# Low words of the first weight's float64 numbers: the shift moved from VectorE to ScalarE

## Chip, core and metric

The kernel runs on one core of a Trainium2 chip. Its engines are TensorE (PE, with PEld for its weight loads), VectorE (DVE), ScalarE (ACT), GpSimd (POOL) and SyncE (SP, which here only issues DMAs). The metric is the device time of one execution in microseconds (us), as the median of several runs; smaller is better.

## What is computed

Causal attention with a bias from a running sum, then two dense two-layer blocks, each 512 to 2048 to 512 wide, over 2304 tokens:

```python
x = attention(q, k, v, s)                 # 4 batches, 8 heads, 576 tokens, head size 64
x = x.transpose(0, 2, 1, 3).reshape(2304, 512)
h = x @ moe_w_in;   x = (h * tanh(log1p(exp(h)))) @ moe_w_out
h = x @ moe2_w_in;  return (h * sigmoid(1.702 * h)) @ moe2_w_out
```

The four weight matrices are handed over as float64. Chip engines work in float32 here, so every weight has to be converted on the core from its two 32-bit words.

## The kernel before

**Stages.** The attention is cut into steps, each for some heads of one tile of 128 queries. `tick()` writes one step: scores on TensorE (L328, L333), their minimum with the bias on VectorE (`do_max`, L346), the exponential on ScalarE (`do_exp`, L358, shown as L112 because the helper `lut` records it), a high and a low half (`do_hilo`, L372 on ScalarE, L373 on VectorE), a transposing DMA (L377), and four steps later the product with v on TensorE (L397, L401). While the attention goes on, the matmuls of the first layer (L581 to L583, `first_layer`) are mixed in for each 256 tokens that are ready. They need the first weight, `moe_w_in`. After the attention come the second layer, then the second block's two layers.

**Loading a weight.** `load_w` is called 16 times for each of the four matrices, once for each 128 columns (or rows). One call issues one DMA of 512 KB into a raw tile `wst` (L543 for an "in" weight). The raw tile is seen as pairs of 32-bit words: `zi` is the low word of each float64, `yi` the high word, `y` the high word read as float32; each is 128 x 512 with a stride of two. For the first weight (`sided` is true) the steps are:

- L562, ScalarE (shown as L112 with the tile wst): the high word is scaled by 2^-112, with a Prelu whose slope for negative numbers sets the sign apart.
- L565, VectorE: the low word is shifted right by 29 bits, so that three bits are left.
- L566, VectorE: the high word is shifted left by three and joined with these three bits.
- L576, ScalarE: the high half of the weight, `th`. L577, GpSimd: the low half, `tl_`, by a subtraction.

The three other weights are not `sided`; they take a Copy (L564) in the place of the Prelu and one more VectorE step (L570). 

**Order.** All engines take their instructions in order. The order on each engine and the buffers are drawn up by a planner when the program is built, and it works from its own model of what each instruction costs (`schedule_with_timeline_sim=True`). The first weight's DMAs are kept behind the transposing DMA written just ahead of them (L547, L548). The 16 loads of the first weight are started by `bg_a`, from `tick` loops and from `first_layer`. Raw tiles of this stage come from the same five buffers (`mo_a`, tag `hs`) that hold the first layer's output on its way to memory.

Of the kernel before, what the change touches and what calls it, by code (L numbers as in the profile page):

```python
# [13 lines left out]
AF = mybir.ActivationFunctionType  # L14
ALU = mybir.AluOpType
# [36 lines left out]
def attention_moe_moe_kernel(  # L52
# [12 lines left out]
    nc = tc.nc  # L65
# [9 lines left out]
    scale = 1.0 / math.sqrt(D)  # L75
# [35 lines left out]
    def lut(out, in_, func, **kw):  # L111
        i = nc.scalar.activation(out=out, in_=in_, func=func, **kw)  # L112
        if gate_ins[0] is not None:
            tc.add_manual_dep(i.ins, gate_ins[0].name, order, reason="table set")
        since.append(i.ins)
        return i
# [11 lines left out]
    def tmp_pair(dt, nm):  # L128
        tmp_n[0] += 1
        p = mo_a if mo_b[0] is None or tmp_n[0] % (MA + MBB) < MA else mo_b[0]  # L130
        return p.tile([128, 1024], dt, tag="hs", name=nm)
# [396 lines left out]
    def load_w(pool, stage, lay, m, kind):  # L528
        t = pool.tile([128, 2, DM], F32R, tag="w", name="w")
        if stage:  # L530
            rt = stage.tile([128, 1024], F32, tag="wst", name="wst", bufs=NRAW)
        else:
            rt = tmp_pair(F32, "wst")
        if wide:
            rv = rt.bitcast(I32)
            r = rv.rearrange("p (f two) -> p f two", two=2)
            src = (w1_in, w2_in, w1_out, w2_out)[lay + 2 * (kind == "out")].bitcast(I32)
        else:
            rv = r = rt[:, 0:DM]
            src = (w1_in, w2_in, w1_out, w2_out)[lay + 2 * (kind == "out")]  # L540
        if kind == "in":
            n = src.shape[1] // NF
            ld = nc.sync.dma_start(  # L543
                out=rv.rearrange("p (c f) -> p c f", c=KC),
                in_=src[:, m * n:(m + 1) * n].rearrange("(c p) f -> p c f", p=128),
            )
            if lay == 0 and last_pt[0] is not None:  # L547
                tc.add_manual_dep(ld.ins, last_pt[0].ins.name, order, reason="weights behind transposes")  # L548
            win_t[lay, m] = t
        else:  # L550
            nc.sync.dma_start(out=rv, in_=src[m * 128:(m + 1) * 128, :])
            wout_t[lay, m] = t
        th, tl_ = t[:, 0, :], t[:, 1, :]
        if not wide:
            nc.scalar.activation(out=th, in_=r, func=AF.Copy)
            nc.vector.tensor_tensor(out=tl_, in0=r, in1=th, op=ALU.subtract)
            return
        zi, yi = r[:, :, 0], r[:, :, 1]
        y = yi.bitcast(F32)
        sided = lay == 0 and kind == "in"  # L560
        if sided:
            lut(y, y, AF.Prelu, scale=2.0 ** -112, alpha=-(2.0 ** 32))  # L562
        else:
            nc.scalar.activation(out=y, in_=y, func=AF.Copy, scale=2.0 ** -112)  # L564
        nc.vector.tensor_scalar(out=zi, in0=zi, scalar1=29, scalar2=None, op0=ALU.logical_shift_right)  # L565
        nc.vector.scalar_tensor_tensor(  # L566
            out=yi if sided else zi, in0=yi, scalar=3, in1=zi, op0=ALU.logical_shift_left, op1=ALU.bitwise_or
        )
        if not sided:
            nc.vector.scalar_tensor_tensor(  # L570
                out=yi, in0=yi, scalar=-(2 ** 31), in1=zi, op0=ALU.bitwise_and, op1=ALU.bitwise_or
            )
        if lay == 0 and kind == "out":
            nc.gpsimd.tensor_scalar(out=th, in0=y, scalar1=1.0, scalar2=0.0, op0=ALU.mult, op1=ALU.add)  # L574
        else:
            nc.scalar.activation(out=th, in_=y, func=AF.Copy)  # L576
        nc.gpsimd.tensor_tensor(out=tl_, in0=y, in1=th, op=ALU.subtract)  # L577
# [7 lines left out]
    def l1_mm(ps, lay, m, xr, first):  # L585
# [15 lines left out]
        out=maskb, in_=maskb, pattern=[[-1, 128]], compare_op=ALU.is_ge, fill=BIG, base=0, channel_multiplier=1  # L601
    )
    nc.gpsimd.memset(maskp, 0.0)
    for a in range(2):
        nc.gpsimd.affine_select(
            out=maskp[64 * a:64 * a + 64], in_=maskp[64 * a:64 * a + 64], pattern=[[-1, 64]],
# [16 lines left out]
    def bg_a():  # L623
        if wq:
            load_w(wa_p, None, 0, wq.pop(0), "in")
# [41 lines left out]
    def bg_w(pool, stage, lay, m, kd):  # L667
        return lambda: load_w(pool, stage, lay, m, kd)
# [76 lines left out]
    for m in range(NF):  # L745
# [7 lines left out]
        if m % 2:  # L753
            nc.sync.dma_start(
                out=h_d[:, m - 1:m + 1, (NU - UE) * U:NT], in_=t.rearrange("p (m t) -> p m t", m=2)
# [11 lines left out]
    for i, (u, t0, W, m0, n) in enumerate(groups1):  # L767
# [20 lines left out]
        if m0 + n == NF:  # L788
            k_ = 512 // W
            for e in range(KC * W // 512):  # L790
# [4 lines left out]
                for p in range(2):  # L795
                    nc.sync.dma_start(
                        out=x2_d[:, p, cs, t0:t0 + W],
                        in_=x2[:, p].bitcast(F32).rearrange("p (c t) -> p c t", c=k_),
# [105 lines left out]
```

## Time and profile before

| | |
|---|---|
| Median of 3 runs | 1065.03 us |
| Lowest, highest run | 1063.39 us, 1070.41 us |
| Profiled execution, its own time | 1066.92 us |
| Its span, first to last instruction | 1065.1 us |
| Granted TensorE clock, mean over the span | 0.962 |
| Busy: PE, DVE, ACT, POOL | 999.0, 557.4, 484.5, 273.3 us |

The profile is of one execution. Its time is 1.82 us more than its span. Times in the trace are counted from the start of the span. Busy time of an engine is the time in which it ran at least one instruction; the granted clock is a share of full speed, so 0.50 is the lower of TensorE's two levels, 1.2 GHz, and 1.00 is 2.4 GHz.

### The profile page before, as it was taken

Reading aid. Unit: us, or ns where it says so; the run is one execution under the profiler, and the core shown is the slowest. Engines: PE = TensorE matmul, PEld = TensorE weight load, DVE = VectorE, ACT = ScalarE, POOL = GpSimd, SP = SyncE. Lnnn points to the kernel's source line nnn. Section 1 sums busy time; section 2 is a strip of 40 time slices with the busy share of each in tenths; the row PEclk is TensorE's granted clock in tenths of the full one; section 3 lists DMA queues with packets and bytes.
Section 4 is the critical chain, followed back from the end, with each engine's and each line's share of the span. In section 5 each row is a group of like instructions: output and inputs, shape, how many; then the busy total and the mean of one; then the engine's idle time right before and its main releaser. Section 6 shows DMA issues by size and latency. Waiting matters only on the chain.

```text
span 1065.1 us, 16948 instructions
## 1 busy us (share of the span) xinstructions
PE 999.0 (94%) x6396; PEld 865.6 (81%) x6396; DVE 557.4 (52%) x1074; ACT 484.5 (45%) x1010; POOL 273.3 (26%) x307
## 2 busy tenths in 40 slices
PE   3688899989999999999999979899999999999998
PEld 3577798888989889987888869688888888888897
DVE  5798786674557863576534575662222222222231
ACT  4778777584658862463212343442222222222121
POOL 3445532341124112655232254220000100100000
PEclk7679899989999999999999989899999999999999
DMA  9899987996699796797533656520300300210010
GB/s 231 161 251 277 258 208 172 231 188 161 139 222 219 146 196 198 251 382 276 178 119 119 194 166 195 158 80 6 114 1 0 99 20 1 60 40 1 20 40 20
DMA packets 192562, 154.35 MB, mean 145 GB/s; under 512 B 117921, under 2 KB 161953, under 8 KB 192481
## 3 DMA queue, kind: packets, MB, share of 16 engines
q1 hardware_dynamic: 182240, 131.25, 46.6%
q0 software_dynamic: 10240, 22.03, 8.1%
q8 instruction: 50, 0.82, 0.3%
q14 instruction: 32, 0.25, 0.1%
HBM read 93.92 MB, written 33.10 MB: 119 GB/s over the span
## 4 chain that ended last, share of the span: by engine, by line
PE 55%; DMA 10%; DVE 5%; POOL 3%; issue 2%; ACT 2%; SPq 0%; ACTq 0%; POOLq 0%; DVEq 0%
PE acc L844 18%; PE h L581 9%; PE h L582 9%; PE h L583 9%; DMA wst<-in_moe_w_out_dram 3%; DMA wst<-in_moe_w_in_dram 2%; POOL w L577 2%; PE s L328 2%; DVE wst L570 2%; PE acc L583 2%; PE acc L582 2%; PE acc L581 2%; DMA hg<-h_d 2%; DVE wst L566 1%; PE o L397 1%
## 5 line engine op out<-in xcount | busy, mean ns | idle before, releaser
L581 PE MATMUL h<-xh,w 128*128 128x256 f32 (+1 forms) x768 | 252.5, 331 | 8.5 <-DVE z L831 5.1
L582 PE MATMUL h<-xh,w 128*128 128x256 f32 (+1 forms) x768 | 248.4, 324 | 0.0
L583 PE MATMUL h<-xh,w 128*128 128x256 f32 (+1 forms) x768 | 246.9, 322 | 0.0
L844 PE MATMUL acc<-w,gh 128*128 128x512 f32 x576 | 177.8, 390 | 0.0
L581 PEld LDWEIGHTS h<-xh,w 128*128 128x128 f32 x768 | 147.6, 193 | 21.3 <-DVE z L831 5.5
L582 PEld LDWEIGHTS h<-xh,w 128*128 128x128 f32 x768 | 148.1, 193 | 10.8
L583 PEld LDWEIGHTS h<-xh,w 128*128 128x128 f32 x768 | 147.5, 192 | 10.5 <-POOL w L577 0.2
L831 DVE TENSOR_TENSOR z<-h,sg 128x512 f32<-128x512 f32 x72 | 49.7, 690 | 193.1 <-ACT sg L112 192.7
L112 ACT ACTIVATE sg<-h 128x512 f32<-128x512 f32 x72 | 42.9, 596 | 204.2 <-PE h L583 204.2
L844 PEld LDWEIGHTS acc<-w,gh 128*128 128x128 f32 x576 | 107.6, 188 | 21.7
L582 PE MATMUL acc<-gl,w 128*128 128x512 f32 (+1 forms) x320 | 120.1, 375 | 4.0 <-DVE gl L717 4.0
L581 PE MATMUL acc<-gh,w 128*128 128x512 f32 (+1 forms) x320 | 119.7, 374 | 3.1 <-POOL w L574 1.7
L577 POOL TENSOR_TENSOR w<-wst,w 128x512 fp32r<-128x512 f32 x64 | 90.6, 1418 | 116.7 <-ACT w L576 115.6
L583 PE MATMUL acc<-gh,w 128*128 128x512 f32 (+1 forms) x320 | 117.6, 374 | 0.7 <-POOL w L577 0.7
L844 PE MATMUL acc<-w,gl 128*128 128x512 f32 x288 | 112.2, 389 | 0.0
L112 ACT ACTIVATE P<-P,mx 128x128 f32<-128x128 f32 (+4 forms) x144 | 83.4, 580 | 33.0 <-DVE mx L346 32.1
L328 PE MATMUL s<-kw,qw 128*128 128x288 f32 (+4 forms) x384 | 90.0, 347 | 7.3 <-DVE kw L175 3.7
L373 DVE SCALAR_TENSOR_TENSOR hl<-P,hl 128x512 f16<-128x512 f32 (+2 forms) x104 | 73.1, 703 | 29.7 <-ACT hl L372 29.4
L809 POOL DMA_DIRECT2D xh<-x_d x20 | 14.5, 727 | 284.2 <-PE h L583 196.2
L833 DVE TENSOR_TENSOR gl<-z,gh 128x512 fp32r<-128x512 f32 x72 | 50.4, 701 | 49.4 <-ACT gh L832 34.9
L346 DVE CUSTOM_DVE_ANT_0 P<-s,ck 128x128 f32<-128x128 f32 (+3 forms) x128 | 59.3, 485 | 31.7 <-PE s L333 30.6
L582 PEld LDWEIGHTS acc<-gl,w 128*128 128x128 f32 x320 | 61.4, 192 | 15.1 <-DVE gl L717 4.8
(90 smaller groups left out, 1723.7 us busy)
## 6 DMA issues: line engine op xcount, KB each, us to landing
h_d<-hs SPq DMA_DIRECT2D x36, 512.0 KB, 4.6
hg<-h_d SPq DMA_DIRECT2D x36, 512.0 KB, 6.4
wst<-in_moe_w_in_dram SPq DMA_DIRECT2D x32, 512.0 KB, 4.8
wst<-in_moe_w_out_dram SPq DMA_DIRECT2D x32, 512.0 KB, 3.9
x_d<-x SPq DMA_DIRECT2D x36, 256.0 KB, 2.4
xh<-x_d POOLq DMA_DIRECT2D x16, 512.0 KB, 5.5
vl<-in_v_dram SPq DMA_DIRECT2D x12, 384.0 KB, 5.4
cp<-cum_d SPq DMA_DIRECT2D x16, 288.0 KB, 5.1
```

Of the source, the lines that this page charges most:

```text
L112: i = nc.scalar.activation(out=out, in_=in_, func=func, **kw)
L328: nc.tensor.matmul(out=o, lhsT=qw[b, i, g][:, hl, w, :], rhs=kw[b, g][:, hl, c0:c1], start=(e == a == w == 0), stop=False, skip_group_chec ...
L346: nc.vector.tensor_tensor_reduce(out=p[:, e * L + c0:e * L + c1], in0=x["S"][f][:, e * L:e * L + c1 - c0], in1=c[:, c0:c1], scale=1.0, sca ...
L373: nc.vector.scalar_tensor_tensor(out=hv[:, 1, 0:wl], in0=x["P"][:, 0:wl], scalar=PSC, in1=hv[:, 0, 0:wl], op0=ALU.mult, op1=ALU.subtract)
L570: nc.vector.scalar_tensor_tensor(out=yi, in0=yi, scalar=-(2 ** 31), in1=zi, op0=ALU.bitwise_and, op1=ALU.bitwise_or)
L577: nc.gpsimd.tensor_tensor(out=tl_, in0=y, in1=th, op=ALU.subtract)
L581: nc.tensor.matmul(out=outp, lhsT=hi_w, rhs=hi_x, start=start, stop=False, skip_group_check=True)
L582: nc.tensor.matmul(out=outp, lhsT=hi_w, rhs=lo_x, start=False, stop=False, skip_group_check=True)
L583: nc.tensor.matmul(out=outp, lhsT=lo_w, rhs=hi_x, start=False, stop=stop, skip_group_check=True)
L831: nc.vector.tensor_tensor(out=z, in0=ps, in1=sg, op=ALU.mult)
L833: nc.vector.tensor_tensor(out=gl, in0=z, in1=gh, op=ALU.subtract)
L844: nc.tensor.matmul(out=acc[tb], lhsT=gx[:, ts], rhs=w[:, wx, :], start=m == 0 and a == 0, stop=m == NF - 1 and a == 2, skip_group_check=True,)
```

## The change

For the first weight alone, the shift of the low word is done on ScalarE. The word is read as an unsigned integer, multiplied by 2^-29 (1 - 2^-6), moved by -0.383 and written back as an integer. The conversion on writing gives a whole number from 0 to 7, the place of the three bits that the shift left. The other weights keep the shift on VectorE.

```diff
@@ load_w
         else:
             nc.scalar.activation(out=y, in_=y, func=AF.Copy, scale=2.0 ** -112)
-        nc.vector.tensor_scalar(out=zi, in0=zi, scalar1=29, scalar2=None, op0=ALU.logical_shift_right)
+        if sided:
+            nc.scalar.activation(
+                out=zi, in_=zi.bitcast(mybir.dt.uint32), func=AF.Copy, bias=-0.383, scale=2.0 ** -29 * (1 - 2.0 ** -6)
+            )
+        else:
+            nc.vector.tensor_scalar(out=zi, in0=zi, scalar1=29, scalar2=None, op0=ALU.logical_shift_right)
         nc.vector.scalar_tensor_tensor(
             out=yi if sided else zi, in0=yi, scalar=3, in1=zi, op0=ALU.logical_shift_left, op1=ALU.bitwise_or
         )
```

## Rows read from the trace of the kernel before

**Rows 1.** The page: busy us, share of the span, instructions of each engine.

```profile
PE 999.0 (94%) x6396; PEld 865.6 (81%) x6396; DVE 557.4 (52%) x1074; ACT 484.5 (45%) x1010; POOL 273.3 (26%) x307
```

**Rows 2.** Windows: stretch, length, busy us by engine (instructions), granted clock, DMA share, GB/s.

```profile
720.00:1065.00 345.00, 341.12 (x1595) 286.01 (x1593) 90.51 (x131) 80.46 (x131) 10.03 (x14) 1.00 0.10 33
...
46.00:125.00 79.00, 66.36 (x553) 56.44 (x553) 71.25 (x160) 64.36 (x149) 42.56 (x46) 0.85 1.11 270
...
50.00:70.00 20.00, 15.89 (x96) 13.18 (x96) 19.12 (x34) 15.05 (x36) 10.66 (x10) 0.58 1.13 240
...
74.00:125.00 51.00, 43.58 (x411) 37.29 (x409) 44.20 (x107) 42.77 (x100) 29.73 (x34) 0.97 1.10 284
...
130.00:140.00 10.00, 10.00 (x97) 9.51 (x97) 7.28 (x20) 9.53 (x29) 4.02 (x6) 0.91 0.64 159
```

**Rows 3.** The tile wst, 30 to 140 us: durations ns min/median/max, first and last start.

```profile
L565 DVE TENSOR_SCALAR wst<-wst x16: 371/422/1537, 46.9 to 121.9; 128x512 int32<-128x512 int32 x16
L112 ACT ACTIVATE wst<-wst x16: 650/676/694, 46.9 to 123.0; 128x512 f32<-128x512 f32 x16
L566 DVE SCALAR_TENSOR_TENSOR wst<-wst x16: 641/688/1327, 47.9 to 124.1; 128x512 int32<-128x512 int32 x16
```

**Rows 4.** Groups by shape, 46 to 125 us: busy us, mean ns, idle before.

```profile
L565 DVE TENSOR_SCALAR wst<-wst 128x512 int32<-128x512 int32 x16 | 8.5, 529 | 0.9 <-DMA wst<-in_moe_w_in_dram 0.7
...
L112 ACT ACTIVATE P<-P,mx 128x512 f32<-128x512 f32 x8 | 5.8, 720 | 1.0 <-DVE mx L346 1.0
...
L653 ACT ACTIVATE hs<-h 128x512 f32<-128x512 f32 x7 | 4.1, 590 | 0.8 <-DMA h_d<-hs 0.7 <-DVE vm L219 0.2
```

**Rows 5.** Timeline of ScalarE: start us, us, instruction.

```profile
46.88 0.68 ACT L112 ACTIVATE wst<-wst 128x512 f32<-128x512 f32 x1
47.45 0.59 ACT L174 ACTIVATE kw<-kt 128x512 fp32r<-128x512 f32 x1
```

**Rows 6.** Timelines of VectorE (shifts and one follower) and GpSimd (one row).

```profile
51.72 0.41 DVE L565 TENSOR_SCALAR wst<-wst 128x512 int32<-128x512 int32 x1
...
57.50 0.41 DVE L565 TENSOR_SCALAR wst<-wst 128x512 int32<-128x512 int32 x1
57.83 0.54 DVE L346 CUSTOM_DVE_ANT_0 P<-s,ck 128x384 f32<-128x384 f32 x1
...
66.79 0.42 DVE L565 TENSOR_SCALAR wst<-wst 128x512 int32<-128x512 int32 x1
...
74.31 0.37 DVE L565 TENSOR_SCALAR wst<-wst 128x512 int32<-128x512 int32 x1
...
105.88 1.54 DVE L565 TENSOR_SCALAR wst<-wst 128x512 int32<-128x512 int32 x1
...
121.93 0.43 DVE L565 TENSOR_SCALAR wst<-wst 128x512 int32<-128x512 int32 x1
...
105.54 1.60 POOL L577 TENSOR_TENSOR w<-wst,w 128x512 fp32r<-128x512 f32 x1 [0.20 <-ACT w L576]
```

**Rows 7.** Waits of ScalarE and VectorE, 46 to 125 us: us, times, longest.

```profile
ACT P L112 <- DVE mx L346: 5.7, 6, 1.4
ACT w L576 <- DVE wst L566: 2.9, 5, 1.8
ACT wst L112 <- DMA wst<-in_moe_w_in_dram: 2.5, 4, 1.0
...
DVE qw L189 <- ACT qw L188: 2.6, 3, 1.6
DVE hl L373 <- ACT hl L372: 1.4, 2, 0.9
```

**Rows 8.** Waits of TensorE, 40 to 130 us, and its timeline at three L581.

```profile
PE o L397 <- DMA pt<-hl: 6.1, 4, 3.5
...
PE h L581 <- ACT w L576: 2.2, 2, 1.4
...
60.79 0.79 PE L581 MATMUL h<-xh,w 128*128 128x256 f32 x2 [0.85 <-ACT xh L442]
...
105.51 0.39 PE L581 MATMUL h<-xh,w 128*128 128x256 f32 x1 [0.81 <-ACT w L576]
...
128.49 0.58 PE L581 MATMUL h<-xh,w 128*128 128x256 f32 x1 [1.37 <-ACT w L576]
```

**Rows 9.** Timeline of TensorE where its clock rises.

```profile
63.63 0.42 PE L581 MATMUL h<-xh,w 128*128 128x256 f32 x1
...
67.23 0.28 PE L581 MATMUL h<-xh,w 128*128 128x256 f32 x1
```

**Rows 10.** Transfers from 40 to 130 us: share of the 16 engines' time by queue.

```profile
q1 hardware_dynamic: 36859, 20.37, 97.7%
```

## The prediction

> **What bounds the kernel now.** I read the page first. TensorE is busy for 94% of the span and VectorE, from which the change takes work, for 52% [rows 1]. Over the whole span a microsecond of VectorE is worth nothing, so the question is where the 16 instructions stand. The view of the tile wst gives it: all 16 shifts start between 46.9 and 121.9 us [rows 3]. That is the stage in which attention steps and the first matmuls of the first layer run side by side. The windows come next. From 46 to 125 us VectorE is busy for 71.25 of 79 us, ScalarE for 64.36 and TensorE for 66.36, at a mean clock of 0.85 [rows 2]. So TensorE stands still for 12.6 us here, and VectorE is the fullest engine, with ScalarE 7 us behind. From 130 us TensorE is full (10.00 of 10), and in the last 345 us it is busy for 341 [rows 2]. What this stage gains or loses therefore reaches the end of the kernel almost whole, unless a later wait takes it up; and what there is to gain is the 12.6 us and some time at the lower clock.
>
> The stage is not all of one kind. From 50 to 70 us VectorE is busy for 19.12 of 20 us, ScalarE for 15.05. From 74 to 125 us it is 44.20 and 42.77 of 51, nearly level [rows 2]. The waits say the same. ScalarE's largest is for VectorE's minimum ahead of an exponential, 5.7 us in 6 waits; VectorE waits for ScalarE too, 2.6 us ahead of qw and 1.4 us ahead of the low half [rows 7]. The attention step is a chain through both, and the transposing DMA stands behind it: TensorE's largest wait in the stage is for that, 6.1 us [rows 8]. The transfers are full as well, the hardware queue's packets taking 97.7% of the engines' time [rows 10], which speaks for a small effect of any engine's change.
>
> **What goes.** Sixteen shifts on VectorE. Their group has 8.5 us of busy time [rows 4], with a median of 422 ns and a longest of 1537 [rows 3]. A plain one occupies the queue less than it lasts: one starts at 57.50 and the next instruction at 57.83, 0.33 us later [rows 6]. The longest ran from 105.88 to 107.42 beside GpSimd's subtraction, 105.54 to 107.14 [rows 6]; such stalls are the difference between 8.5 us and 16 x 0.422 = 6.8 us, 1.7 us in all, and they go too, if their place isn't taken by another VectorE instruction. VectorE's relief is thus 16 x 0.33 = 5.3 us at least and 8.5 us at most. Also gone is that VectorE waits for a weight's DMA at the shift, 0.7 us once [rows 4].
>
> **What comes.** Sixteen Copies with scale and bias on ScalarE, 128 x 512, stride two, integer in and out. No row has ScalarE reading or writing integers. The nearest is the Prelu on the other word of the same tile, in place, with the same stride: median 676 ns [rows 3]. The bounds are 590 ns, the first layer's plain Copy from PSUM, and 720 ns, the exponential of the same size with a bias that is read from memory [rows 4]. I take the Prelu's. Start to start it is 0.57 us, since ScalarE's next instruction begins before it ends (46.88, then 47.45) [rows 5]. So ScalarE gets 16 x 0.57 = 9.1 us of queue time; between 16 x 0.48 = 7.7 and 16 x 0.61 = 9.8 us, by the bounds less the same overlap of 0.11. A cost below zero is excluded, because nothing on ScalarE is removed. It has 79 - 64.36 = 14.6 us of idle time in the stage, of which 5.7 are waits for VectorE's minimum that may themselves shrink.
>
> On the Trainium skill: the page "ScalarE: Activation LUTs", in its rules for kernel authors, advises VectorE and not ScalarE for additions and products, because VectorE is the faster per element. The trace agrees in kind, 422 against 676 ns [rows 3], so the move makes total engine work larger. The same page, under what ACT_TABLE_LOAD costs, puts an activation with constants for scale and bias at 186 ns + 0.833 ns per element, 612 ns for 512; by it the sum below would have 16 x 0.50 = 8.0 us in the place of 9.1, an estimate from that page, and the forecast would be 0.5 us lower. The Prelu's row is 64 ns above that figure, and the row decides.
>
> **What is moved.** For each weight, the two words were treated side by side, the shift on VectorE and the Prelu on ScalarE. Now they follow each other on ScalarE and the join (L566) comes 0.57 us later at the earliest, then the high half (L576) and the low half. No DMA moves in the text. Queued on ScalarE behind the new instruction are exponentials, kT and qT copies and the high halves of the attention, whose VectorE and TensorE partners wait for them.
>
> **The sum.** Three terms, by stretch.
> - 50 to 70 us: five shifts start here, the first at 51.72, the last at 66.79, at 0.41 or 0.42 us [rows 6]. VectorE sets the pace (19.12 of 20) and ScalarE's 4.95 us of idle time covers the 5 x 0.57 = 2.9 us that it gets [rows 2]. The gain lies between nothing and 5 x 0.42 = 2.1 us. I take 1.5, as the idle time in front of exponentials is waiting for VectorE. If that cover is gone, the 2.9 us come on top.
> - 74 to 125 us: ten shifts, the first at 74.31, the last at 121.93 [rows 6]. ScalarE goes from 42.77 to 42.77 + 10 x 0.57 = 48.5 of 51 us, and VectorE falls from 44.20 to about 39. The fuller engine's share now is 44.20 / 51 = 0.867; if a stretch lasts as long as its fuller engine at that share needs, it becomes 48.5 / 0.867 = 55.9 us, 4.9 longer. At the other end ScalarE's 8.2 us of idle time take all 5.7 us and nothing is lost. I take the middle, 2.5 longer.
> - TensorE waits twice for the high half of a weight, at 105.51 and 128.49 [rows 8]. Both become 0.57 us longer: 1.1 us. The first weights are hidden: TensorE's first L581 runs at 60.79 and waits for xh, not for a weight [rows 8], some 14 us after the first shift.
>
> The sixteenth shift, at 46.9 us, lies in ScalarE's idle time. The sum is -1.5 + 2.5 + 1.1 = 2.1 us longer, some 2 us. The profiled execution would go from 1066.92 to 1069; it stands 1.9 us above the median of 1065.03, so the median becomes **1067 us**, between 1065.03 - 2.1 = 1063 and 1065.03 + 4.9 + 1.1 = 1071 by the bounds of these terms. A difference under 1% (10.7 us) is about what a measurement of this kernel can't tell from no change.
>
> **The rivals.**
> - *ScalarE becomes the bound, slower.* Every added 0.57 us falls on the attention's chain, because ScalarE is left with some 5 us of idle time in 79. The price is 9.1 us, the 1.1 us of the weights, and what TensorE's clock costs when its gaps lengthen: the matmuls of the first layer last 0.42 us at 63.63, at the lower level, and 0.28 us at 67.23, after it has worked back to back [rows 9]; a dozen more at the lower level are 12 x 0.14 = 1.7 us. Together 11.9: 1077 us. It decides once ScalarE's waits for VectorE's minimum are gone, that is where ScalarE alone sets the pace. For it speaks the level load from 74 us on; against it, that VectorE's relief is nearly as large and that the largest wait of TensorE there is for a transposing DMA. 0.16.
> - *VectorE was the bound throughout, faster.* All 8.5 us go from the chain, and TensorE's steady work starts earlier, with the same 1.7 us or a little more at the higher clock: some 10.7 us, 1054 us. For it: the 90% of VectorE over the stage, and the 5.7 us that ScalarE waits for its minimum. Against it: ScalarE's 81% plus 9.1 us is 93%, more than VectorE has now. 0.12.
> - *The planner draws another order.* The costs that it works from change at 16 places, so instructions after 47 us can be placed otherwise on every engine, outside `load_w` as well; then the time moves by the order and not by the shift. What can be lost or won is TensorE's idle time in the span, 66 us [rows 1], most of it outside this stage; I give it some 10 us to either side, 1055 to 1077, sign unknown. 0.10.
> - *The change doesn't do what it says*: the new instruction takes far longer because of its integers, twice the Prelu, 1.36 us. ScalarE would then have 9.1 + 16 x 0.68 = 20 us more and the stage would grow by at least the 5.4 us over its idle time. This is inside the slower case's time and has no row for it; I count it there.
>
> **How the numbers follow.** The forecast has 0.62. The planner's case is half within 1%, 0.02 faster and 0.03 slower beyond. So within 1%: 0.62 + 0.05 = 0.67; slower: 0.16 + 0.03 = 0.19; faster: 0.12 + 0.02 = 0.14. The range reaches to both rivals' near ends, 1056 to 1077, which leaves out something under 2 in 10.
>
> **What would show each step.** In the changed profile, L565 is gone from this stage, and a new line of ScalarE on wst has 16 with a mean near 0.68 us. From 46 to 125 us VectorE's busy time is near 63 us and ScalarE's near 74. ScalarE's waits for the minimum shrink below 5.7 us, VectorE's for ScalarE grow above the 4.0 us of rows 7, and the two waits of TensorE for a high half lengthen. TensorE's idle time in the stage stays near 12.6 us. I am wrong if that idle time moves by more than some 6 us, if the new instruction's mean is well outside 0.59 to 0.72 us, or if the difference arises where no first weight is loaded, after 130 us, which would be the order's doing.

## The result, and the profile after

The changed kernel takes 1074.56 us (median of 20 runs, 1064.72 to 1082.23). The kernel before took 1066.51 us in 20 runs (1063.39 to 1074.53). The ratio is 1.0064, with an interval of 1.0043 to 1.0086: some 6.8 us slower. The ratio is taken over undisturbed runs and isn't the quotient of the two medians. The forecast was 2.1 us slower and "within 1%"; it is within 1%, but the loss is about three times the sum, and clear of the noise of 20 runs. The profiled execution's span goes from 1065.1 to 1075.4 us, 10.3 us more.

The page of the changed kernel, busy time by engine. Against [rows 1], ScalarE has 16 instructions more and VectorE 16 fewer, as the text of the change says:

```profile
PE 997.4 (93%) x6396; PEld 863.5 (80%) x6396; DVE 554.6 (52%) x1058; ACT 491.9 (46%) x1026; POOL 275.4 (26%) x307
```

In the changed text the new ScalarE shift is L566, the join L571, the copy of the high half L581 and GpSimd's subtraction L582; the first layer's three matmuls are L586 to L588. The view of the tile wst, from 30 to 145 us:

```profile
L112 ACT ACTIVATE wst<-wst x16: 652/677/696, 45.5 to 129.1; 128x512 f32<-128x512 f32 x16
L566 ACT ACTIVATE wst<-wst x16: 635/671/692, 46.0 to 129.7; 128x512 int32<-128x512 uint32 x16
L571 DVE SCALAR_TENSOR_TENSOR wst<-wst x16: 680/692/1190, 46.7 to 130.5; 128x512 int32<-128x512 int32 x16
...
L581 ACT ACTIVATE w<-wst x16: 648/662/679, 49.1 to 135.6; 128x512 fp32r<-128x512 f32 x16
```

The new instruction costs what the forecast took for it. But the last Prelu stands at 129.1 us, where it was at 123.0 [rows 3]: the whole stage runs late. Its windows (columns as in [rows 2]):

```profile
46.00:125.00 79.00, 60.59 (x482) 51.13 (x482) 60.00 (x132) 65.06 (x150) 37.10 (x39) 0.86 1.04 242
...
46.00:140.00 94.00, 70.03 (x568) 59.23 (x566) 68.15 (x156) 75.68 (x180) 45.06 (x48) 0.85 1.02 238
...
50.00:70.00 20.00, 14.43 (x106) 11.87 (x106) 15.28 (x23) 15.24 (x35) 9.17 (x9) 0.81 0.98 209
...
74.00:125.00 51.00, 39.10 (x330) 33.73 (x330) 37.52 (x94) 43.06 (x100) 23.81 (x27) 0.90 1.06 251
...
130.00:140.00 10.00, 4.43 (x23) 3.79 (x22) 4.22 (x18) 5.62 (x19) 3.22 (x4) 0.66 0.89 183
...
140.00:400.00 260.00, 248.22 (x2353) 226.69 (x2352) 172.67 (x461) 181.52 (x461) 70.94 (x98) 0.98 0.86 186
```

Two of these stretches, the second and the last, were not shown of the kernel before:

```profile
46.00:140.00 94.00, 79.46 (x661) 68.68 (x662) 81.31 (x193) 76.84 (x187) 49.00 (x54) 0.83 1.06 256
...
140.00:400.00 260.00, 250.04 (x2392) 228.19 (x2391) 171.55 (x454) 179.62 (x448) 67.89 (x94) 0.98 0.87 187
```

From 46 to 140 us TensorE stands still for 94 - 70.03 = 24.0 us, where it was 14.5. These 9.4 us are nearly as much as the 10.3 us of the span; from 140 to 400 us another 1.8 us of idle time is added. (Both profiles are single executions, and executions of one program differ by as much; what the change costs is the 0.64% of the 20 runs.) Of the 9.4 us, 3.9 arise before 130 us and 5.6 from 130 to 140 us, where TensorE had no idle time before [rows 2]. In the stretch from 46 to 140 us TensorE does 568 matmuls where it did 661. No engine is full in the stage any more: from 46 to 125 us VectorE has 60.00 of 79 us, ScalarE 65.06, which is hardly more than the 64.36 before, although it has 16 instructions to do more: it gets through 150 in these 79 us, and it was 149. So an engine that has too much work isn't what the windows show; they all wait more. The granted clock is not the reason either: 0.86 against 0.85 in these 79 us.

Who waits for whom. The waits of ScalarE and VectorE are those from 46 to 125 us, the waits of TensorE those from 40 to 130 us (us in total, times, longest):

```profile
ACT wst L112 <- DMA wst<-in_moe_w_in_dram: 5.4, 4, 2.5
ACT P L112 <- DVE mx L346: 4.7, 4, 2.2
...
DVE wst L571 <- ACT wst L566: 3.8, 2, 2.1
DVE hl L373 <- ACT hl L372: 3.2, 5, 1.4
...
DVE qw L189 <- ACT qw L188: 1.1, 2, 0.6
...
PE o L397 <- DMA pt<-hl: 15.6, 10, 4.4
```

TensorE's wait for the transposing DMA was 6.1 us in 4 waits [rows 8]. Now it is 15.6 us in 10. That isn't all lost: up to 130 us TensorE's idle time as a whole grew by 3.9 us only, as other waits became shorter. ScalarE's wait for a weight's DMA went from 2.5 us [rows 7] to 5.4 us. Both are waits for transfers, and no transfer was changed.

That pointed to the order of the instructions. The built programs can be compared place by place, without any time. Apart from the shift itself, planning gave TensorE another instruction at 500 of its 6396 places, VectorE at 110 of 898, ScalarE at 127 of 865, GpSimd at 29 of 307 and SP's queue at 11 of 354. All of TensorE's are between its places 194 and 828, which is this stage. It can be seen in the timeline of TensorE. Before, a score matmul at 62.15 came ahead of the block of first-layer matmuls:

```profile
62.15 1.01 PE L328 MATMUL s<-kw,qw 128*128 128x384 f32 x2
62.97 0.33 PE L333 MATMUL s<-maskb,identb 128*128 128x128 bf16 x1
63.05 0.56 PE L582 MATMUL h<-xh,w 128*128 128x256 f32 x1
```

After, 24 of the first layer's come first, from 59.84, and the scores wait behind them until 63.37. The last row is the last weight of the first layer, for which TensorE stood still for 5.55 us:

```profile
59.84 0.56 PE L586 MATMUL h<-xh,w 128*128 128x256 f32 x1
...
63.25 0.28 PE L588 MATMUL h<-xh,w 128*128 128x256 f32 x1
63.37 0.52 PE L328 MATMUL s<-kw,qw 128*128 128x384 f32 x2
...
136.25 0.58 PE L586 MATMUL h<-xh,w 128*128 128x256 f32 x1 [5.55 <-ACT w L581]
```

That wait isn't the shift's doing. On ScalarE's timeline the copy that TensorE waited for stands behind an attention step that waited 4.38 us for a DMA:

```profile
134.75 0.42 ACT L150 ACTIVATE qraw<-qraw 128x256 f32<-128x256 f32 x1 [4.38 <-DMA qraw<-in_q_dram]
135.07 0.58 ACT L174 ACTIVATE kw<-kt 128x512 fp32r<-128x512 f32 x1
135.55 0.65 ACT L581 ACTIVATE w<-wst 128x512 fp32r<-128x512 f32 x1
```

### The profile page after: what moved, and what is told of

The parts are those of the page before. It is cut to its first block, busy times and chain, and to the rows that moved or that the text cites. A ratio compares the mean times of both kernels' runs of the same rounds, so it can differ in the third digit from the quotient of the medians.

```text
span 1075.4 us, 16944 instructions
## 1 busy us (share of the span) xinstructions
PE 997.4 (93%) x6396; PEld 863.5 (80%) x6396; DVE 554.6 (52%) x1058; ACT 491.9 (46%) x1026; POOL 275.4 (26%) x307
## 4 chain that ended last, share of the span: by engine, by line
PE 53%; DMA 9%; DVE 6%; POOL 4%; issue 3%; ACT 2%; SPq 0%; ACTq 0%; POOLq 0%; DVEq 0%
PE acc L849 18%; PE h L586 8%; PE h L587 8%; PE h L588 8%; DMA wst<-in_moe_w_out_dram 3%; DMA wst<-in_moe_w_in_dram 3%; POOL w L582 2%; DVE wst L575 2%; PE acc L588 2%; PE s L328 2%; PE acc L587 2%; PE acc L586 2%; DVE wst L571 1%; DMA kraw<-in_k_dram 1%; DVE gl L722 1%
## 5 line engine op out<-in xcount | busy, mean ns | idle before, releaser
L586 PE MATMUL h<-xh,w 128*128 128x256 f32 (+1 forms) x768 | 252.6, 331 | 12.9 <-DVE z L836 6.4
L588 PE MATMUL h<-xh,w 128*128 128x256 f32 (+1 forms) x768 | 248.0, 324 | 0.9 <-POOL w L582 0.9
L586 PEld LDWEIGHTS h<-xh,w 128*128 128x128 f32 x768 | 147.9, 194 | 25.5 <-DVE z L836 6.8
L588 PEld LDWEIGHTS h<-xh,w 128*128 128x128 f32 x768 | 148.5, 193 | 11.9 <-POOL w L582 1.3
L586 PE MATMUL acc<-gh,w 128*128 128x512 f32 (+1 forms) x320 | 118.9, 372 | 2.4 <-POOL w L579 1.2
L582 POOL TENSOR_TENSOR w<-wst,w 128x512 fp32r<-128x512 f32 x64 | 90.0, 1408 | 119.6 <-ACT w L581 118.5
L588 PE MATMUL acc<-gh,w 128*128 128x512 f32 (+1 forms) x320 | 116.7, 371 | 0.7 <-POOL w L582 0.7
L814 POOL DMA_DIRECT2D xh<-x_d x20 | 14.5, 726 | 285.4 <-PE h L588 197.3
L397 PE MATMUL o<-v,pt 128*128 128x128 f16 (+2 forms) x480 | 53.9, 228 | 25.2 <-DMA pt<-hl 24.9
```

What stands on the lines that cost most here:

```text
L397: nc.tensor.matmul(out=o[rows, j % 4, :], lhsT=t[:kn, e * nb + kb, rows], rhs=vv, start=(kb == 0 and j % 4 == 0), stop=False, skip_group_c ...
L586: nc.tensor.matmul(out=outp, lhsT=hi_w, rhs=hi_x, start=start, stop=False, skip_group_check=True)
L588: nc.tensor.matmul(out=outp, lhsT=lo_w, rhs=hi_x, start=False, stop=stop, skip_group_check=True)
```

## The experiments

Two theories. *Theory O (order)*: the 16 instructions cost about what the sum of the forecast says, and the rest of the loss is the order that the planner drew anew. *Theory S (shift)*: the work that was moved costs the whole loss, and a new order is only its shadow. To tell them apart, the order of each engine is written into the kernel, as a list of the places of its instructions in the program's text. Each instruction is tied to the one ahead of it on its engine, by an edge that orders and adds no semaphore:

```diff
+def _pin(tc):
+    every = list(tc._region_blocks()[0].instructions)
+    edge = mybir.DependencyInfo(mybir.DependencyClass.NoSync, mybir.DependencyReason.DATA)
+    for seq in _j.loads(_z.decompress(_b.b64decode(_ORDER))):
+        for a, c in zip(seq, seq[1:]):
+            tc.add_manual_dep(every[c], every[a].name, edge, reason="written order")
...
         attention_moe_moe_kernel(tc, *args)
+        _pin(tc)
```

All ratios below are to the kernel before, run again on the same chip beside them.

### The order and the shift, each alone

**e1: the changed kernel in the order of the kernel before.** The edit is the one above, with the old order; each ScalarE shift stands right behind the Prelu of its weight.

> The changed kernel's instructions, but every engine takes them in the order of the kernel before, written out by hand; each ScalarE shift stands right behind its Prelu, where the changed kernel has it too. Theory O (the order that the planner redrew costs the 0.64%): this is within 0.3% of the kernel before, 1064 to 1070 us, and TensorE waits for the transposing DMA about 6 us in the stage, as before. Theory S (the work on ScalarE costs it, whatever the order): 0.4 to 0.9% slower than before, 1071 to 1076 us.

Measured: 1066.73 us against 1063.66, ratio 1.0027 (0.9998 to 1.0056), some 2.9 us.

**e2: the kernel before in the order of the changed one.** The same edit on the old text; each VectorE shift stands right ahead of its join.

> The kernel before, its shifts on VectorE, but every engine takes its instructions in the order of the changed kernel; each shift stands right ahead of its join on VectorE. Theory O: still 0.4 to 0.9% slower than before, 1071 to 1076 us. Theory S: within 0.3% of the kernel before.

Measured: 1073.83 us, ratio 1.0084 (1.0053 to 1.0115), some 8.9 us. None of the 16 instructions has moved to ScalarE, and the loss is there. The windows and TensorE's largest wait in e1, then in e2:

```profile
46.00:125.00 79.00, 65.73 (x547) 56.47 (x546) 60.40 (x137) 69.99 (x162) 42.13 (x45) 0.86 1.10 267
...
46.00:140.00 94.00, 78.07 (x647) 67.94 (x647) 70.08 (x170) 82.17 (x200) 49.05 (x54) 0.85 1.05 252
...
PE o L397 <- DMA pt<-hl: 5.9, 5, 2.3
```

```profile
46.00:125.00 79.00, 59.73 (x450) 50.61 (x451) 65.46 (x147) 57.57 (x133) 37.69 (x39) 0.85 1.00 239
...
46.00:140.00 94.00, 70.29 (x567) 59.76 (x567) 76.12 (x174) 68.71 (x165) 46.02 (x48) 0.86 1.00 240
...
PE o L397 <- DMA pt<-hl: 12.9, 7, 5.1
```

In e1, ScalarE is fuller than in the changed kernel (69.99 us against 65.06), and yet TensorE is busy for 78.07 of the 94 us, 1.4 less than before. In e2 ScalarE has only 57.57 us, and TensorE is busy for 70.29, as in the changed kernel (70.03). So TensorE's idle time follows the order and not the engine that shifts. Theory O holds, and it is e2 that decides: Theory S had it within 0.3% of the kernel before, while e1's interval reaches into what either theory expected. The long wait for the last weight comes with the order too. In e2 the copy of its high half stands behind the same kind of attention step (ScalarE, then TensorE):

```profile
135.62 0.42 ACT L150 ACTIVATE qraw<-qraw 128x256 f32<-128x256 f32 x1 [3.33 <-DMA qraw<-in_q_dram]
...
137.12 0.48 PE L581 MATMUL h<-xh,w 128*128 128x256 f32 x1 [3.97 <-ACT w L576]
```

From 130 to 140 us TensorE is busy for 10.00 us in e1, as before, and for 5.57 us in e2.

One control is missing. The changed kernel with its own order written out, and nothing else changed, was not run, so a cost of the writing itself isn't excluded in the new order: all its written kernels stand at 1.0082 or above, the changed kernel at 1.0064. Against it speak e12 below, which shows none in the old order, and that e2's TensorE has 567 matmuls from 46 to 140 us, as the changed kernel's has 568 without a written order. The two effects don't add up (0.27 and 0.84% apart, 0.64% together); the intervals are too wide to say whether the shift's cost vanishes in the new order or the runs only scatter.

**e3: the old order, with a second ScalarE instruction behind each shift.** It prices ScalarE's share by itself: 16 more of the same size, and nothing taken from VectorE for them.

```diff
+            nc.scalar.activation(out=zi, in_=zi, func=AF.Copy)
```

> As the first of these kernels (old order, shift on ScalarE), with one more ScalarE instruction of the same size behind each shift, a Copy of the low word onto itself, which leaves the values as they are. It doubles the load on ScalarE. Theory S: it adds once more what the first kernel lost, 1.0 to 1.6% slower than before in all. Theory O: ScalarE has some 14 us of idle time in the stage and takes most of it; at most 0.5% slower than before.

Measured: 1072.55 us, ratio 1.0086 (1.0054 to 1.0119). That is 5.8 us above e1's median of 1066.73, 0.36 us for each added instruction; it is more than Theory O put on record (at most 0.5% altogether), and less than Theory S did (1.0 to 1.6%), whose low end the interval reaches. ScalarE's time in this stage isn't free: 0.36 us of some 0.57 us come through, if the added Copy costs only by its time on ScalarE; it also puts off the join behind it. If the 16 shifts of e1 cost 5.8 us as well, then, as e1 is only 2.9 us slower, VectorE's relief gives about 2.9 us back; that the first sixteen cost what the second do is assumed, not shown. By the intervals of e1 and e3 each of these figures is uncertain by some 4 us to either side. In e3's windows ScalarE is busy for 75.09 of 79 us, the fullest that any engine was here:

```profile
46.00:125.00 79.00, 62.41 (x479) 53.15 (x478) 56.66 (x133) 75.09 (x167) 38.58 (x40) 0.81 1.01 242
...
L569 ACT ACTIVATE wst<-wst x16: 651/668/695, 47.5 to 131.5; 128x512 int32<-128x512 int32 x16
```

### The terms of the sum

The forecast's sum had a gain for the early shifts and a loss for the late ones. These runs move the two parts one by one.

**e4: shifts 7 to 16 on ScalarE, the planner free.**

```diff
-        if sided:
+        if sided and m >= 6:
```

> Only the last ten loads of the first weight have the shift on ScalarE; the planner is free and draws an order that differs from both. Theory O: the time is that of another draw, anywhere from 0.7% faster to 1% slower than before, not between the two kernels by the count of shifts. Theory S: 10/16 of the loss, 0.3 to 0.6% slower.

Measured: 1069.08 us, ratio 1.0040 (1.0018 to 1.0063). The planner drew a third order, so this run can't tell order from work; both theories allow it.

**e5: the first six on ScalarE, old order** (`if sided and m < 6`, and the old order written in).

> The old order, written out; only the first six loads of the first weight have the shift on ScalarE, the other ten keep it on VectorE. Theory T (the two terms of the sum are real: where VectorE sets the pace the move gains, where both are level it loses): 2 to 4 us faster than before, 0.2 to 0.4%, and the ninth load's DMA is issued about 3 us earlier than before. Theory U (every moved shift costs alike): 6/16 of the loss of all sixteen in that order, 0.1% slower.

Measured: 1065.68 us against 1064.93, ratio 1.0005 (0.9973 to 1.0038). A gain isn't seen, though Theory T's smallest, 0.2%, lies inside the interval. The ninth load's DMA is issued at 76.83 us, 2.3 us earlier than before (79.15); but in e6, which leaves the first six on VectorE, it is issued at 76.96, so that is no sign of a gain.

**e6: the last ten on ScalarE, old order** (`if sided and m >= 6`).

> The old order; only the last ten loads have the shift on ScalarE. Theory T: 4 to 7 us slower than before, 0.4 to 0.7%, more than all sixteen in that order cost. Theory U: 10/16 of what all sixteen cost, 0.2% slower.

Measured: 1067.38 us, ratio 1.0033 (1.0000 to 1.0066), some 3.5 us. By the middle values the late shifts carry e1's whole loss. But the intervals of e5 and e6 hold what Theory U expected (0.1% and 0.2%) as well as the near ends of Theory T, so the two theories aren't told apart.

### Which part of the new order costs

**e7 and e8: ScalarE's waits for weights.** In the changed kernel four Prelus stood at the head of ScalarE's queue and waited 5.4 us for their weights; attention work stood behind them. *Theory Q (queue)*: these are the loss. In e7 the Prelu and shift of the sixth and seventh load come five places later on ScalarE and their joins four later on VectorE, and those of the ninth and tenth three places later on both (the expectation says five and four of all four pairs); the rest of the new order is kept. The edit is in the list of places alone:

```diff
+# four pairs of Prelu and shift, and their joins, later in ScalarE's and VectorE's lists
-_ORDER = "..."
+_ORDER = "..."
```

> The changed kernel in its own order, with one difference: the four pairs of Prelu and shift that stood waiting for their weight's DMA (loads 6, 7, 9 and 10) are put five places later on ScalarE, behind attention instructions that were ready, and their joins four places later on VectorE. Theory Q (the new order loses because attention work stands behind weights that haven't landed): ScalarE's 5.4 us of waits for weights between 66 and 97 us fall to under 2, and the time is 3 to 6 us below the changed kernel, 0.1 to 0.4% over before. Theory R (the loss of the new order is spread over all engines' places): no change from the changed kernel, 0.5 to 0.8% over before.

Measured: 1073.27 us, ratio 1.0082 (1.0051 to 1.0114). The wait for weights fell from 5.4 to 2.6 us, and nothing was won. But ScalarE now waits for a join at the copy of the high half, which the changed kernel doesn't (waits of ScalarE from 46 to 125 us, e7):

```profile
ACT w L581 <- DVE wst L571: 3.8, 2, 2.4
ACT wst L112 <- DMA wst<-in_moe_w_in_dram: 2.6, 3, 2.0
```

e8 is the same with three places for all four, on both engines, in case five was too late:

> As the one before, three places later on both engines. Theory Q: between the changed kernel and the one before, 0.2 to 0.6% over before. Theory R: as the changed kernel.

Measured: 1075.8 us, ratio 1.0109 (1.0063 to 1.0154). The same waits in e8:

```profile
ACT w L581 <- DVE wst L571: 4.5, 3, 2.5
...
ACT wst L112 <- DMA wst<-in_moe_w_in_dram: 0.7, 1, 0.7
```

The four Prelus' places are not what costs the time: their waits went almost wholly and the kernel became no faster. Theory Q falls in that form. That ScalarE is held up by a weight at all is not excluded, since most of the wait came back at the high half, 4.5 us of it in e8.

**e9 to e12: SP's queue.** Here the new order sends one transposing DMA behind two loads of a weight. SP's queue before, then after:

```profile
66.93 1.34 SPq L377 DMA_TRANSPOSE pt<-hl  x1
68.91 0.93 SPq L543 DMA_DIRECT2D wst<-in_moe_w_in_dram  x2
```

```profile
69.00 0.33 SPq L218 DMA_DIRECT2D vl<-in_v_dram  x1
69.42 2.61 SPq L543 DMA_DIRECT2D wst<-in_moe_w_in_dram  x2
72.15 1.21 SPq L377 DMA_TRANSPOSE pt<-hl  x1
```

*Theory V (SP's queue)*: this is why TensorE waits for transposes. e9 is the changed kernel in the new order with SP's queue as before:

> The changed kernel in its own order on four engines, but SP's queue in the order of the kernel before (the two differ in 11 of SP's 354 places). Theory V (the new order loses because a transposing DMA stands behind two weight DMAs in SP's queue, which wait for raw buffers): 4 to 8 us below the changed kernel, 0 to 0.4% over before; the transposing DMA that the changed kernel issues at 72 us goes out by 68. Theory R (the loss is spread over the other engines' places, TensorE's above all): no change, 0.5 to 0.9% over before.

Measured: 1072.95 us against 1063.48, ratio 1.0082 (1.0055 to 1.0108). In e9's trace the transposing DMA goes out ahead of the loads again, but at 69.50 and not at 66.93; TensorE waits less for transposes and longer for VectorE's half of k (3.7 us before, 1.9 in the changed kernel), and its busy time to 140 us is still low:

```profile
69.50 1.22 SPq L377 DMA_TRANSPOSE pt<-hl  x1
70.81 1.08 SPq L543 DMA_DIRECT2D wst<-in_moe_w_in_dram  x2
...
PE o L397 <- DMA pt<-hl: 8.8, 7, 3.3
PE s L328 <- DVE kw L175: 6.3, 2, 5.2
...
46.00:140.00 94.00, 70.82 (x568) 59.42 (x569) 68.96 (x155) 75.86 (x180) 44.95 (x48) 0.81 1.01 235
```

The DMA is late although nothing new stands ahead of it in the queue, so the queue's order isn't what makes it late. e10 is the kernel before with SP's queue of the changed one:

> The converse: the kernel before in its own order on four engines, SP's queue in the order of the changed kernel. Theory V: 0.4 to 0.8% slower than before. Theory R: within 0.3% of before.

Measured: 1065.9 us, ratio 1.0027 (1.0003 to 1.0051). In e11 (the changed kernel in its new order) only the one displaced transposing DMA goes back ahead of the two loads of weights; in e12 (the kernel before) only this one is moved behind them:

> The changed kernel in its own order; only one transposing DMA goes back to its old place in SP's queue, ahead of a v load and two weight DMAs. Theory V: as the kernel with the whole old SP queue, 0 to 0.4% over before. Theory R: no change from the changed kernel.

Measured: 1077.22 us, ratio 1.0117 (1.0094 to 1.0141). It went out hardly earlier than the changed kernel's 72.15, and the weights behind it later (SP's queue in e11):

```profile
71.21 1.21 SPq L377 DMA_TRANSPOSE pt<-hl  x1
72.51 1.08 SPq L543 DMA_DIRECT2D wst<-in_moe_w_in_dram  x2
```

> The kernel before in its own order; only that one transposing DMA is put behind the v load and the two weight DMAs, as the changed kernel has it. Theory V: 0.3 to 0.8% slower than before, by this single place. Theory R: within 0.3% of before.

Measured: 1064.05 us, ratio 1.0004 (0.9982 to 1.0026). To put the DMA back made it no better, to displace it cost nothing. Theory V falls as the main cause: its share is e10's 0.27%, 0.51% at the end of its interval. e12 also says that writing out the old order costs nothing that can be measured here.

The runs in one table. TensorE's busy time is that of the window from 46 to 140 us in each profiled execution:

| Kernel | order | shift on ScalarE | ratio | TensorE busy, us |
|---|---|---|---|---|
| before | old | none | 1 | 79.46 |
| e12 | old, one DMA moved | none | 1.0004 | 75.97 |
| e5 | old | first six | 1.0005 | 79.01 |
| e10 | old, new SP queue | none | 1.0027 | 79.20 |
| e1 | old | all | 1.0027 | 78.07 |
| e6 | old | last ten | 1.0033 | 77.23 |
| e4 | a third | last ten | 1.0040 | 74.34 |
| after | new | all | 1.0064 | 70.03 |
| e9 | new, old SP queue | all | 1.0082 | 70.82 |
| e7 | new, pairs 5 and 3 later | all | 1.0082 | 70.41 |
| e2 | new | none | 1.0084 | 70.29 |
| e3 | old | all, and 16 more | 1.0086 | 73.88 |
| e8 | new, pairs 3 later | all | 1.0109 | 70.63 |
| e11 | new, one DMA back | all | 1.0117 | 67.99 |

Every kernel in the new order has 68 to 71 us, every kernel in the old one without added work 76 to 79. The matmuls done in that window differ alike: 550 to 568 in the new order, 647 to 662 in the old. From 130 to 140 us alone TensorE is busy for 3.0 to 5.6 us in every kernel of the new order and for all 10.00 in every one of the old without added work. No version that was run beats the kernel before.

## Why the forecast was right in kind and short in size

- **Where it counts.** The stage is right. That a loss there reaches the end almost whole fits the two profiles (9.4 us of TensorE's idle time, 10.3 us of span), but single executions can't show it: e6's profiled execution has a span of 1073.3 us, 8.2 more than before, with only 2.2 us more idle time in this stage.
- **The new instruction.** Right: a median of 671 ns, where the Prelu's 676 [rows 3] stood for it, and integers cost nothing extra. The Trainium skill's page "ScalarE: Activation LUTs", under what ACT_TABLE_LOAD costs, would give 612 ns, an estimate that the forecast worked out from it; the measured row stands 59 ns above it.
- **The sum.** Not contradicted for what it summed: 2.1 us were forecast, and the moved work in an unchanged order measured 2.9 us (e1; -0.2 to 6.0 by its interval). By terms: the late shifts and TensorE's weight waits were 2.5 + 1.1 = 3.6 us, and e6 measured 3.5; as its interval goes from 0 to 7 us, so close a match is luck. The early shifts' gain of 1.5 us was not seen (e5: 0.5 us longer, between 2.9 shorter and 4.0 longer). It was argued from a VectorE that was busy for 19.12 of 20 us [rows 2]; but e3 shows that queue time on ScalarE is paid for as well, so relief of the one and load of the other may largely cancel; that is argued.
- **The step that failed** is the planner's rival: "some 10 us to either side", sign unknown, with a chance of 0.10. It is what happened, with 0.84% (0.53 to 1.15) from the order alone in e2. The forecast summed the change on the old order, which the changed kernel doesn't have, and so put the order at nothing in its sum. The mechanism was named and its chance was far too small: the planner redrew the order both times that it was free to (the changed kernel and e4). Its size was about right, but by a weak argument: the 66 us of TensorE's idle time limit what an order can win, not what it can lose. That the time stayed within 1% is luck in part, since the order's interval lies across that line.
- **ScalarE as the bound** (1077 us) lies near the measured time, and isn't its cause. ScalarE was to reach 74 us of 79; it has 65.06. Its waits for VectorE's minimum are not gone (4.7 us, 5.7 before), and e2 loses as much with a ScalarE that is relieved. Only e3, with twice the added work, comes to that state.
- **The signs.** VectorE's busy time was to be near 63 us and is 60.00; its waits for ScalarE were to grow beyond 4.0 and are 3.8 + 3.2 + 1.1 = 8.1 us, nearly all of the growth at the join, which is new; a wait of TensorE for a high half did lengthen, to 5.55 us, but for a DMA of q. TensorE's idle time from 46 to 125 us was to stay near 12.6 us, wrong beyond some 6 us; it is 18.4, 5.8 more, just inside. The last sign, a difference after 130 us, did show itself: 5.6 of the 9.4 us are from 130 to 140 us. It was drawn badly all the same. In the changed kernel the last weight is still being converted then, and the orders differ in the very stage where the shifts are, so the place of a difference could not tell order from work. Only a run with a fixed order could.

What stays open is which places of the new order cost the time. SP's queue (e9 to e12) and the places of the four waiting pairs (e7, e8) are excluded as the main cause. Two things fit the rows, but are argued and not shown: the block of 24 first-layer matmuls ahead of scores, with what follows from it for the transposes, and the copy of the last weight's high half behind an attention step that waits for q, where TensorE stands still for 2.5 to 7.0 us in the kernels of the new order. Neither TensorE's order alone nor that one place on ScalarE was tried. The planner also assigns buffers; whether it did so otherwise with the new order was not compared.

## What to carry to other kernels

Where a planner orders the instructions, an edit of 16 instructions is an edit of the whole stage: compare the order before and after, and run the new work in the old order and the old work in the new one before explaining a difference. In this stage, in which two engines are nearly level, moving work from the fuller one to the other bought nothing that could be measured (e1: 0.27% slower, between nothing and 0.56%). A rival whose rough size is known and whose sign isn't should have the chance that its cause occurs, and here the cause occurred both times.

## What had not been expected

- ScalarE reads unsigned and writes signed integers at no extra time: 671 ns against 677 ns for floats of the same shape and stride in the same kernel.
- An instruction added to ScalarE cost 0.36 us of its 0.57 us of queue time (e3 against e1, uncertain by more than half of it), although ScalarE had 79 - 69.99 = 9 us of idle time in the stage: here the idle time of an engine that stands in a chain with others was only partly cover.
- One and the same program scatters by more than the change: 1063.39 to 1074.53 us over 20 runs of the kernel before. The span of a single profiled execution can therefore mislead by more than the effect, while TensorE's busy time in the stage told the two orders apart in every profile but e3's, whose added work lowers it too.
- The order of the instructions alone, with none moved to another engine, cost more than the moved work did: 0.84% (e2) against 0.27% (e1).
